# Sums of a weight pair ahead of its last parts, conversion steps of ScalarE one step later, other PSUM banks at both ends of the channel layer, one product moved

## Chip, cores and metric

One core of one Trainium2 chip runs the whole program. The metric is the device time of one execution in microseconds (us), the median of several runs.

## The reference, cut to what matters

Three layers follow each other: attention with a computed position bias, a token and channel mixer, and a gated mixer. The change lies in the second and in the conversion of weights around it.

```python
def _moe_ref(x, w_tok1, w_tok2, w_ch1, w_ch2):        # x: 4 x 576 x 512
    xt = x.transpose(0, 2, 1)
    h = np.maximum(xt @ w_tok1, 0.0) @ w_tok2          # token mixing, 576 -> 256 -> 576
    u = x + h.transpose(0, 2, 1)
    h2 = np.maximum(u @ w_ch1, 0.0) @ w_ch2            # channel layer, 512 -> 1536 -> 512
    return u + h2
```

The third layer, `_moe2_ref`, begins with `x @ w_in` and ends with `@ w_out`.

## The kernel before

**Numbers in two parts.** Every large product works on operands that are split into a high part (rounded to the matmul format `F32R`) and a low part (the remainder). A product is three matmuls for each 128 rows of contraction: high by high, high by low, low by high. ScalarE (ACT) makes the high part by a cast, VectorE (DVE) the low part by a subtraction.

**Weights.** They come as 64-bit numbers. `Jobs` (L70) converts them, one block of 128x512 at a time, while the products run. A job is a row of pieces: the square of the upper word on ScalarE (L158, into the one buffer `sq`), then four steps of DVE on the words (L159, L165, L170, L175), of which L175 reads `sq`. Between these steps stand the high part (`finish`, L122 on ScalarE) and the low part (`subtract`, L132 on DVE) of the job before. `piece()` issues one such step; `work(k)` issues k of them at fixed places of the channel layer, and `wjobs.limit` says how far they may run ahead. `need(key)` issues what is missing at once. Each engine works off its own queue in order.

**The channel layer** runs over 2304 columns of `X`, as a first double of 2 x 512 columns with 256 more beside it (`d0`, `small=True`) and a second double of 2 x 512 columns (`d1`). A double goes over the 1536 hidden features in six pairs of blocks of 128, in three groups of two; below they are called pair 0 to pair 5 (n in `Double.run`, L1350). A pair uses seven half products in place of eight, in a scheme after Strassen and Winograd: on the weights' side it wants the blocks themselves (`wa`, `wq`, `wb`) and four sums of them (`wsum`, made by `sum_steps`, L969, with the name `ws`), on the columns' side four mixed blocks M1 to M4 (`mixer`, L1470: subtractions of DVE, then casts of ScalarE and subtractions of DVE again) and M22.

In a pair n > 0 of the first double TensorE (PE) runs, in this order: the product of `wa` with the first half of u into bank `ma`, which ScalarE copies to `s1` (L1370); the product with the second half into `mb`, which DVE adds to `s1` (L1386); the product of `ws` (S2) with M2, added to `ma`, which ScalarE copies (L1390); the 256 columns (`up256`, L1260); S1 with M1 into `mb` (up to pair 4, and in pair 5 too before the change); S3 with M3 into `ma`, copied by L1411; M4 into `ma`; the 256 columns' second product (`down256`, L1281, banks `my` and `mx`); S4 with M22. Between them stand the second products of the pair before (`down1`, L1228, into four banks `a`). In pairs 2 and 4, where a group begins, the group before is closed: `close` adds its sums to `X` (L1236), and `other` runs the second products of its other half, from the parts that `relu` makes (L1070 on ScalarE, L1074 on DVE). Pair 0 has code of its own (`pair0`, L1327).

The bodies `hooks0` and `hooks1` say at which places of a pair the mixers, the weight pieces and the fetches come. SyncE (SP) issues all DMAs: the loads of the raw weights (two buffers), the stores of `wa`, `wb` and `ws` to DRAM for the second double (L953), and their fetches.

**Around it.** Token mixing of the last batch ends with products `pu` (L1099), which DVE adds to `X` (L1104). The gated mixer begins with products `pv` (L1615).

Of the kernel before, what the change touches and what calls it, by code (L numbers as in the profile page):

```python
# [19 lines left out]
def kernel(ctx, tc, ins, consts, out, dbg=None, nb=4, stop=None):  # L20
# [49 lines left out]
    class Jobs:  # L70


        def __init__(self, stg, ahead):
            self.stg, self.ahead = stg, ahead
            self.queue, self.loaded, self.next, self.open, self.gen = [], {}, 0, None, None
            self.done = set()
            self.rest = None
            self.lnext, self.limit, self.last = 0, None, {}
# [57 lines left out]
        def parts(self):  # L136

            self.load()
            key, src, wd, dst, times = self.queue[self.next]
            self.next += 1  # L140
            if src is None:
                for i, step in enumerate(dst):
                    if i > 0:
                        yield
                    step()
                self.done.add(key)
                return
            raw = self.loaded.pop(self.next - 1)
            n = src.shape[1] * src.shape[2]
            r = slice(0, src.shape[0] * times)  # L150
            if wd:
                w = self.stg.tile([P, WMAX], F32, tag="w", name="w", bufs=2)
                sq = self.stg.tile([P, WMAX], F32, tag="sq", name="sq", bufs=1)
                self.subtract()
                up_, dn = raw[r, 0:n, 1], raw[r, 0:n, 0]
                wf = w[r, 0:n]
                wi_ = wf.bitcast(I32)
                S.activation(out=sq[r, 0:n], in_=up_.bitcast(F32), func=AF.Square)  # L158
                V.tensor_scalar(  # L159
                    out=wi_, in0=up_, scalar1=0x07FFFFFF, scalar2=3,  # L160
                    op0=ALU.bitwise_and, op1=ALU.logical_shift_left,
                )
                yield
                self.finish()
                V.scalar_tensor_tensor(  # L165
                    out=wi_, in0=up_, scalar=-0x40000000, in1=wi_, op0=ALU.bitwise_and, op1=ALU.bitwise_or
                )
                yield
                self.subtract()
                V.scalar_tensor_tensor(  # L170
                    out=wi_, in0=dn, scalar=29, in1=wi_, op0=ALU.logical_shift_right, op1=ALU.bitwise_or
                )
                yield

                V.scalar_tensor_tensor(  # L175
                    out=wf, in0=sq[r, 0:n], scalar=THR * THR, in1=wf, op0=ALU.is_ge, op1=ALU.mult
                )
            else:
                self.finish()
                self.subtract()  # L180
                wf = raw[r, 0:n]
            self.open = (key, wf, dst)
            self.last[key] = wf
# [782 lines left out]

    S1, S3, S4, S2 = range(4)

    def sum_steps(j):  # L969
# [17 lines left out]
        def one():  # L987
            wjobs.finish()
            new_s(j)
            raw.append(stg.tile([P, WMAX], F32, tag="sq", name="sq").rearrange("p (o a b) -> p o a b", o=2, a=ND2))  # L990
            (a11, a12), (a21, a22) = w(2 * j), w(2 * j + 1)
            add(0, a21, a22, ALU.add)
            add(1, a11, a21)
            hi(S1)

        def two():
            wjobs.subtract()

        def three():
            lo(S1)  # L1000
            (a11, a12), (a21, a22) = w(2 * j), w(2 * j + 1)
            add(1, raw[0][:, 0], a11)
            add(0, a12, raw[0][:, 1])
            hi(S4)
            if j < NJ - 2:
                keep("a", j, wa[j])
                keep("b", j, wb[j])

        def four():
            lo(S4)  # L1010
            if j < NJ - 1:
                keep("s", j, wsum[j])

        return [one, two, three, four]

# [200 lines left out]
    with tc.tile_pool(name="ps_ch", bufs=1, space=PSUM, reuse_waits="tile") as pc:  # L1216
# [73 lines left out]
        class Double:  # L1290
# [36 lines left out]
            def pair0(self):  # L1327

                (j, j1), a, b = self.groups[0], bank("ma"), bank("mb")
                for ps, w, m in ((a, [wa[j][:, i] for i in range(2)], (M1, M2)), (b, None, (M1, M2))):  # L1330
# [18 lines left out]

            def run(self, hooks, first=False, small=False, banks=("ma", "ma", "mb", "mb"), end=None):  # L1350

                self.small, self.hooks = small, hooks
                seq = [(g, j) for g in self.groups for j in g]
                for n, (group, j) in enumerate(seq):
# [15 lines left out]
                    S.copy(out=s1, in_=a)  # L1370
                    step(k_)
                    if da:
                        self.down1(pj, 0, pgrp, range(ND) if small or begins else range(ND2))
                    step(k_)
# [16 lines left out]
                    step(k_)  # L1391
                    if da and not small and not begins:
                        self.down1(pj, 0, pgrp, range(ND2, ND))
                        relu(s1, gs[0])
# [5 lines left out]
                    if begins:  # L1400
# [5 lines left out]
                        else:  # L1406
                            self.other(acc, lst, 1, k_)
                    c = bank(banks[3])
                    product(c, ws_(S1), M1, start=True)
# [14 lines left out]
                    elif n > 0:  # L1424
                        self.down1(pj, 1, pgrp)
                        step(1)
                    product(a, [wb[j][:, i] for i in range(2)], M4)
                    relu(a, gs[1])
                    hooks(n, "P4")
                    if sm and not begins:  # L1430
                        down256(j)
                        relu(s1, gs[0])
                    elif not sm and not begins and (small or not da):
                        relu(s1, gs[0])
# [23 lines left out]
                acc = [bank(nm) for nm in end] if end else new_acc()  # L1458
                for k in range(len(lst)):
                    self.other(acc, lst, k, self.pieces if k + 1 < len(lst) else 0)  # L1460
                    build()
                add_up(acc, self.c0 + CK)

# [29 lines left out]
        def hooks0(n, where):  # L1493
            if where == "start":
                wjobs.limit = base + 5 * (n + 1) + 1
            if where == "up":
                wjobs.limit = base + 5 * (n + 1) + 2
            if n == 0 and where == "others":
                mixer(3, raws(), 0)
                for i in range(2):  # L1500
                    S.copy(out=M22[i], in_=M2[i].bitcast(F32))
                mixer(2, raws(), 0)
            if n == 0 and where == "C21":
                wjobs.limit = base + 8
                work(8)
                mixer(1, slots[2:4], 0)
            if where == "P3":
                wjobs.limit = base + 5 * (n + 1) + 5
                work(4 if n > 0 else 0)
            if n == 0 and where == "P3":  # L1510
                mixer(4, raws(), 0)
            if n < NJ - 1:
                return
            if where == "P7":
                u_parts(D1, u0)
                for i in (3, 2, 4, 1):
# [29 lines left out]

        d0.run(hooks0, first=True, small=True)
        fetch("s", order1[0], new_s(order1[0], 1))
        d1.run(hooks1, banks=("ma", "my", "mb", "mx"), end=("ma", "mb", "mx", "my"))
    mxr.release()  # L1550
# [328 lines left out]
```

## Time and profile before

| what | us |
|---|---|
| median of 3 runs (877.66 to 879.55) | 877.88 |
| the profiled execution | 878.13 |
| its span, first to last instruction | 876.3 |
| PE busy | 848.7 (97%) |
| DVE busy | 698.6 (80%) |
| ScalarE busy | 457.0 (52%) |

The channel layer lies from 358 to 661 us of the span; the first double's pairs 1 to 5 begin with their first product at 375, 403, 438, 458 and 493 us, the second double at 537 us. A busy share of PE says little of what is to be had; its idle time and what ended it is the view to begin with, then the granted clock behind each such wait, then the queue of the engine that ended it.

### The profile page before, as it was taken

Reading aid. Unit: us, or ns where it says so; the run is one execution under the profiler, and the core shown is the slowest. Engines: PE = TensorE matmul, PEld = TensorE weight load, DVE = VectorE, ACT = ScalarE, POOL = GpSimd, SP = SyncE. Lnnn points to the kernel's source line nnn. Section 1 sums busy time; section 2 is a strip of 40 time slices with the busy share of each in tenths; the row PEclk is TensorE's granted clock in tenths of the full one; section 3 lists DMA queues with packets and bytes.
Section 4 is the critical chain, followed back from the end, with each engine's and each line's share of the span. In section 5 each row is a group of like instructions: output and inputs, shape, how many; then the busy total and the mean of one; then the engine's idle time right before and its main releaser. Section 6 shows DMA issues by size and latency. Waiting matters only on the chain.

```text
span 876.3 us, 21629 instructions
## 1 busy us (share of the span) xinstructions
PE 848.7 (97%) x8608; PEld 704.3 (80%) x8608; DVE 698.6 (80%) x1526; ACT 457.0 (52%) x996; POOL 231.8 (26%) x440
## 2 busy tenths in 40 slices
PE   9999999999999999969999899999998999999998
PEld 4466788888888888858787777888877989889997
DVE  7899788888887789589798876467578989988756
ACT  7999888888888635343343333123244522322310
POOL 1345567676766200000000000000003322322230
PEclk9999999999999999989999999999999999999999
DMA  7965544444432132044343010435025001010002
GB/s 190 190 141 132 133 92 77 81 93 87 90 70 62 57 108 97 1 147 165 97 157 120 24 49 26 144 111 202 15 78 109 25 1 49 1 61 1 1 13 97
DMA packets 127732, 74.30 MB, mean 85 GB/s; under 512 B 104592, under 2 KB 112912, under 8 KB 126352
## 3 DMA queue, kind: packets, MB, share of 16 engines
q1 hardware_dynamic: 127472, 72.79, 32.0%
q8 instruction: 68, 1.11, 0.5%
q14 instruction: 32, 0.26, 0.1%
q10 hardware_dynamic: 160, 0.13, 0.1%
HBM read 47.01 MB, written 13.11 MB: 69 GB/s over the span
## 4 chain that ended last, share of the span: by engine, by line
PE 53%; DVE 7%; ACT 2%; issue 1%; DMA 0%; DVEq 0%; ACTq 0%; SPq 0%
PE a L1228 11%; PE ps L1690 6%; PE pu L1668 6%; PE pv L1615 6%; PE po L1721 6%; PE ma L1064 5%; PE mb L1064 3%; PE my L1064 2%; PE mx L1064 2%; PE pu L1099 2%; PE mx L1260 1%; PE ph L674 1%; DVE g L1074 1%; DVE X L1236 1%; PE mx L1281 1%; DVE w L170 1%
## 5 line engine op out<-in xcount | busy, mean ns | idle before, releaser
L530 POOL TENSOR_SCALAR pr<-pr,sm 128x576 f32<-128x576 f32 (+2 forms) x208 | 130.7, 646 | 46.0 <-DVE sm L523 37.8
L1228 PE MATMUL a<-g,c 128*128 128x512 f32 x528 | 125.7, 390 | 1.6 <-ACT c L122 1.3
L1228 PEld LDWEIGHTS a<-g,c 128*128 128x128 f32 x528 | 98.7, 188 | 23.1 <-ACT c L122 1.5
L516 ACT ACTIVATE pr<-pr,mn 128x576 f32<-128x576 f32 x144 | 112.3, 780 | 6.7 <-DVE mn L503 4.2
L503 DVE CUSTOM_DVE_ANT_0 pr<-ss,bias_m 128x576 f32<-128x576 f32 x128 | 94.5, 750 | 19.3 <-PE ss L497 17.4
L63 POOL TENSOR_TENSOR y<-X,y 128x576 fp32r<-128x576 f32 x4 | 7.0, 1787 | 366.0 <-DMA wsr<-in_moe_w_sg_dram 366.0
L597 PEld LDWEIGHTS o<-xA,vm 64*64 64x64 f32 x1280 | 69.9, 133 | 11.1 <-issue 5.4
L597 PE MATMUL o<-xA,vm 64*64 64x128 f32 (+1 forms) x1280 | 78.8, 261 | 0.0
L1183 DVE STREAM_TRANSPOSE res<-X 32x256 f32<-32x256 f32 (+1 forms) x176 | 68.2, 387 | 2.8
L598 PE MATMUL o<-yA,vm 64*64 64x128 f32 x1024 | 68.0, 272 | 0.0
L497 PE MATMUL ss<-kt,X 64*64 64x288 f32 x816 | 66.8, 410 | 0.0
L158 ACT ACTIVATE sq<-wraw 128x512 f32<-128x512 f32 (+2 forms) x43 | 28.2, 655 | 56.7 <-DVE w L175 38.5
L598 PEld LDWEIGHTS o<-yA,vm 64*64 64x64 f32 x1024 | 56.4, 133 | 0.4
L1690 PE MATMUL ps<-wsT,vn 128*128 128x288 f32 x384 | 56.4, 295 | 0.0
L374 DVE TENSOR_SCALAR X<-ttab,wsm 128x576 f32<-128x576 f32 x108 | 55.3, 572 | 0.1
L1690 PEld LDWEIGHTS ps<-wsT,vn 128*128 128x128 f32 x384 | 52.7, 188 | 0.3 <-POOL vn L63 0.2
L1668 PEld LDWEIGHTS pu<-y,c 128*128 128x128 f32 x384 | 51.3, 188 | 0.3
L1668 PE MATMUL pu<-y,c 128*128 128x288 f32 x384 | 51.5, 294 | 0.0
L573 PE MATMUL x<-ident,pr 128*128 128x128 f32 x320 | 47.0, 273 | 0.0
L1721 PE MATMUL po<-u,gm 128*128 128x512 f32 x192 | 44.0, 389 | 0.0
L1721 PEld LDWEIGHTS po<-u,gm 128*128 128x128 f32 x192 | 36.0, 188 | 7.4
L63 POOL TENSOR_TENSOR gm<-uT,gm 128x512 fp32r<-128x512 f32 x16 | 23.3, 1454 | 70.0 <-ACT gm L62 70.0
(257 smaller groups left out, 1977.0 us busy)
## 6 DMA issues: line engine op xcount, KB each, us to landing
wraw<-in_moe_w_ch_dram SPq DMA_DIRECT2D x24, 512.0 KB, 3.6
bias_m<-bst SPq DMA_DIRECT2D x32, 288.0 KB, 3.9
s<-ws SPq DMA_DIRECT2D x5, 1024.0 KB, 4.2
ws<-s SPq DMA_DIRECT2D x5, 1024.0 KB, 5.6
vm<-in_v_dram SPq DMA_DIRECT2D x32, 128.0 KB, 3.1
wraw<-in_moe_w_in_dram SPq DMA_DIRECT2D x8, 512.0 KB, 3.8
out_dram<-res SPq DMA_DIRECT2D x16, 256.0 KB, 2.1
kr<-in_k_dram SPq DMA_DIRECT2D x48, 72.0 KB, 3.0
```

Of the source, the lines that this page charges most:

```text
L497: T.matmul(ss[a % na][o, hf, 0:HN], lhsT=ql, rhs=kr_, start=True, stop=True)
L503: V.tensor_tensor_reduce(out=pr[:, a * NB:a * NB + N].rearrange("p (f n) -> p f n", f=2), in0=ss[a][:, :, 0:HN], in1=bias[a].rearrange("p ...
L516: S.activation(out=pr[:, a * NB:a * NB + N], in_=pr[:, a * NB:a * NB + N], func=AF.Exp, scale=-1.0, bias=mn[:, a:a + 1], accum_out=sm[:, a ...
L530: G.tensor_scalar(out=pr[:, dc:dc + hi - lo], in0=pr[:, lo:hi], scalar1=sm[:, a:a + 1], scalar2=1.0, op0=ALU.mult, op1=ALU.mult,)
L597: T.matmul(o[0:HD, 0:w], lhsT=vm[r, t, 0], rhs=xs[r, t, 0:w], start=st_, stop=en)
L598: T.matmul(o[HD:P, 0:w], lhsT=vm[r, t, 1], rhs=rh[r], start=st_, stop=en)
L1064: T.matmul(ps, lhsT=w[i][:, d], rhs=x[j][:, d], start=start and d == 0 and n == 0, stop=stop and d == ND2 - 1 and n == 2, skip_group_check ...
L1183: V.transpose(out=o, in_=src(c)[32 * a:32 * a + 32])
L1228: T.matmul(acc[d], lhsT=c2[f][i][:, d * P:(d + 1) * P], rhs=g[:, j], start=start and m == 0, stop=stop and m == 2,)
L1668: T.matmul(pu[:, hf, 0:HN], lhsT=wi[i][0][d][:, f * P:(f + 1) * P], rhs=y[j][:, d, js], start=d == 0 and m == 0, stop=d == ND - 1 and m == 2,)
L1690: T.matmul(ps[:, hf, 0:HN], lhsT=vn[i][:, t, ds_], rhs=wsT[j][:, t, js], start=t == 0 and m == 0, stop=False,)
L1721: T.matmul(po[:, cs], lhsT=g[i][:, d, gs], rhs=wo[j][d][:, cs], start=d == 0 and m == 0, stop=d == NG - 1 and m == 2,)
```

## The change

- `sum_steps` has five steps in place of four. The two sums and their high and low parts come first; the high parts (`finish`) and low parts (`subtract`) of `wq` and `wb` come after them. The store of the sums is issued ahead of the stores of `wa` and `wb`.
- From the channel layer on (`wjobs.late`), ScalarE's square is issued with the second step of DVE in place of the first, `finish` with the third in place of the second, `subtract` ahead of the fourth in place of the third.
- At the start of pair 0 all pieces up to the sums of pair 1 are issued, then mixer 3. Mixer 4 moves to pair 1, behind the addition to `s1`.
- The four `a` banks are named first (`new_acc` in `pair0`). They come to lie in PSUM banks 0 to 3 and `ma`, `mb` in 4 and 5; before, `ma` and `mb` lay in 0 and 1, the `a` banks in 2 to 5. The last `pu` of token mixing lies in 4 and 5 in both, and the four buffers of `pv` in 0 to 3.
- In pair 5, S1 goes into bank `mx` in place of `mb`, and half of the `down1` that stood ahead of the second product stands behind S2 (`two`). `need` for the last second-layer block is called at the place P7.
- The last of the four second products of the first double's other half, with its addition to `X`, is handed to the second double, which runs it in its first pair ahead of M4 (`fill`).

```diff
@@ Jobs.parts
-                S.activation(out=sq[r, 0:n], in_=up_.bitcast(F32), func=AF.Square)
+                square = lambda: S.activation(out=sq[r, 0:n], in_=up_.bitcast(F32), func=AF.Square)
+                if not self.late:
+                    square()
...
-                self.finish()
+                late = self.late
+                if late:
+                    square()
+                else:
+                    self.finish()
...
-                self.subtract()
+                if late:
+                    self.finish()
+                else:
+                    self.subtract()
...
+                if late:
+                    self.subtract()
@@ sum_steps
         def one():
-            wjobs.finish()
             new_s(j)
...
         def two():
-            wjobs.subtract()
-
-        def three():
             lo(S1)
...
+        def three():
+            lo(S4)
+            if j < NJ - 1:
+                keep("s", j, wsum[j])
+            summed.add(j)
+
+        def four():
+            wjobs.finish()
+
+        def five():
+            wjobs.subtract()
             if j < NJ - 2:
                 keep("a", j, wa[j])
                 keep("b", j, wb[j])
@@ Double.pair0
+                self.acc = new_acc()
                 (j, j1), a, b = self.groups[0], bank("ma"), bank("mb")
@@ Double.run
+                    two = da and not sm and not begins
                     if da:
-                        self.down1(pj, 0, pgrp, range(ND) if small or begins else range(ND2))
+                        self.down1(pj, 0, pgrp, range(ND2) if two else range(ND))
...
-                    if da and not small and not begins:
+                    if two:
                         self.down1(pj, 0, pgrp, range(ND2, ND))
                         relu(s1, gs[0])
...
-                    c = bank(banks[3])
+                    c = bank(banks[3] if sm else "mx")
...
+                    elif fill is not None:
+                        fill()
                     product(a, [wb[j][:, i] for i in range(2)], M4)
...
-                for k in range(len(lst)):
-                    self.other(acc, lst, k, self.pieces if k + 1 < len(lst) else 0)
+                for k in range(len(lst) - 1):
+                    self.other(acc, lst, k, self.pieces)
                     build()
-                add_up(acc, self.c0 + CK)
+
+                def rest():
+                    self.other(acc, lst, len(lst) - 1)
+                    add_up(acc, self.c0 + CK)
+
+                return rest
@@ hooks0
             if where == "start":
                 wjobs.limit = base + 5 * (n + 1) + 1
+                if n == 0:
+                    wjobs.limit = base + 8
+                    while 1 not in summed:
+                        wjobs.piece()
+                    mixer(3, raws(), 0)
+            if n == 1 and where == "P2":
+                mixer(4, raws(), 0)
...
             if n == 0 and where == "others":
-                mixer(3, raws(), 0)
...
             if n == 0 and where == "C21":
-                wjobs.limit = base + 8
-                work(8)
+                work(2)
                 mixer(1, slots[2:4], 0)
...
-                work(4 if n > 0 else 0)
-            if n == 0 and where == "P3":
-                mixer(4, raws(), 0)
+                work(5 if n > 0 else 0)
...
             if where == "P7":
+                wjobs.need(("c2", NF - 1))
...
+        wjobs.late = True
+        rest = d0.run(hooks0, first=True, small=True)
```

**ScalarE between pair 0 and pair 1.** `g` are the parts of relu, `wq` and `wb` the second block's high parts, `ws` the sums' high parts, `m` the mixers' high parts (from `cs`: mixer 1, from `scratch`: mixer 4), `s` the copy of the first product of pair 1. Before:

```order
L1070 ACTIVATE g_6599<-mx 128x512
L1070 ACTIVATE g_6600<-ma 128x512
L122 CAST wq<-w 128x256
L122 CAST wb<-w 128x256
L981 CAST ws<-sq 128x512 x2
L1466 CAST m_6017<-cs_6603 128x512
L1466 CAST m_6017<-cs_6604 128x512
L1466 CAST m_6607<-scratch 128x512 x2
L1370 COPY s_6019<-ma 128x512
```

And now:

```order
L1084 ACTIVATE g_6596<-mx 128x512
L1084 ACTIVATE g_6597<-ma 128x512
L122 CAST wq<-w 128x256
L122 CAST wb<-w 128x256
L1489 CAST m_6017<-cs_6600 128x512
L1489 CAST m_6017<-cs_6601 128x512
L1385 COPY s_6019<-ma 128x512
L158 ACTIVATE sq<-wraw 128x512 x2
L1489 CAST m_6604<-scratch 128x512 x2
L1406 COPY cs_6600<-ma 128x512
```

The casts of the sums are gone from here (they stand ahead of pair 0's copies), and the copy to `s` stands ahead of mixer 4's casts.

**DVE in pair 5**, from the addition to `s1` on; `c` are low parts of second-layer weights, `u` those of the second double's columns, `cs` what L1412 and L1436 add up. Before:

```order
L1386 TENSOR_TENSOR s_6019<-mb,s_6019 128x512
L132 TENSOR_TENSOR c_10_5988<-w,c_10_5987 128x512
L170 SCALAR_TENSOR_TENSOR w<-wraw,w 128x512
L175 SCALAR_TENSOR_TENSOR w<-sq,w 128x512
L1412 TENSOR_TENSOR cs_6604<-mb,cs_6604 128x512
L63 TENSOR_TENSOR u_5960<-X,u_5959 128x512 x4
```

And now:

```order
L1402 TENSOR_TENSOR s_6019<-mb,s_6019 128x512
L179 SCALAR_TENSOR_TENSOR w<-wraw,w 128x512
L132 TENSOR_TENSOR c_10_5988<-w,c_10_5987 128x512
L185 SCALAR_TENSOR_TENSOR w<-sq,w 128x512
L1088 SCALAR_TENSOR_TENSOR g_6596<-s_6019,g_6596 128x512
L1428 TENSOR_TENSOR cs_6601<-mx,cs_6601 128x512
L132 TENSOR_TENSOR c_11_5990<-w,c_11_5989 128x512
L63 TENSOR_TENSOR u_5960<-X,u_5959 128x512 x4
```

The relu of `s1` and the low part of the last second-layer block come earlier, and the sum is read from `mx`.

## Rows read from the trace of the kernel before

**Rows 1.** Page, part 1: engine, busy us (share of span), instructions.
```profile
PE 848.7 (97%) x8608; PEld 704.3 (80%) x8608; DVE 698.6 (80%) x1526; ACT 457.0 (52%) x996; POOL 231.8 (26%) x440
```
**Rows 2.** PE's waits, whole span: tile, line, releaser: us in total, times, longest.
```profile
PE ma L1064 <- ACT s L1370: 8.3, 1, 8.3
PE mb L1064 <- DVE s L1386: 2.3, 1, 2.3
PE pv L1615 <- DVE X L1236: 2.3, 1, 2.3
PE my L1281 <- DVE c L132: 1.8, 2, 0.9
...
PE a L1228 <- ACT c L122: 1.3, 1, 1.3
PE my L1281 <- ACT g L1070: 1.2, 2, 0.8
...
PE px L658 <- DVE x L63: 0.8, 1, 0.8
...
PE ma L1064 <- ACT cs L1411: 0.7, 1, 0.7
```
**Rows 3.** Stretches: length; busy of PE, PEld, DVE, ACT, POOL; PEclk; DMA share; GB/s.
```profile
360.40:421.30 60.90, 51.01 (x273) 43.74 (x271) 50.04 (x88) 25.65 (x45) 0.00 (x0) 0.94 0.37 121
...
386.20:389.00 2.80, 2.77 (x7) 2.22 (x8) 2.63 (x6) 0.55 (x1) 0.00 (x0) 0.50 0.00 0
...
502.50:505.30 2.80, 2.75 (x7) 2.17 (x8) 1.89 (x3) 0.03 (x1) 0.00 (x0) 0.50 0.00 0
...
520.10:523.40 3.30, 3.19 (x13) 2.34 (x14) 2.71 (x5) 0.00 (x0) 0.00 (x0) 1.00 0.78 303
```
**Rows 4.** PE in order of time: start, us, line, out<-in [idle before <-releaser].
```profile
358.32 2.93 PE L1064 MATMUL ma<-m,wa 128*128 128x512 f32 x12
...
372.14 1.60 PE L1281 MATMUL my<-g,c 128*128 128x256 f32 x12
...
386.23 2.93 PE L1064 MATMUL ma<-m,ws 128*128 128x512 f32 x6 [8.30 <-ACT s L1370]
...
423.72 1.55 PE L1064 MATMUL mb<-m,ws 128*128 128x512 f32 x6
...
502.55 2.92 PE L1064 MATMUL mb<-m,ws 128*128 128x512 f32 x6 [2.27 <-DVE s L1386]
505.28 1.82 PE L1064 MATMUL ma<-m,ws 128*128 128x512 f32 x6
...
520.12 3.38 PE L1228 MATMUL a<-g,c 128*128 128x512 f32 x12 [1.25 <-ACT c L122]
...
544.75 1.66 PE L1064 MATMUL ma<-m,wb 128*128 128x512 f32 x6 [0.68 <-ACT cs L1411]
...
663.60 11.22 PE L1615 MATMUL pv<-c,u 128*128 128x512 f32 x48 [2.25 <-DVE X L1236]
```
**Rows 5.** DVE in order of time, same columns.
```profile
359.13 0.75 DVE L1104 TENSOR_TENSOR X<-pu,X 128x576 f32<-128x576 f32 x1
...
407.88 0.69 DVE L985 TENSOR_TENSOR ws<-sq,ws 128x512 fp32r<-128x512 f32 x1 [0.69 <-ACT ws L981]
...
420.61 0.68 DVE L132 TENSOR_TENSOR c<-w,c 128x512 fp32r<-128x512 f32 x1
```
**Rows 6.** ScalarE in order of time, same columns.
```profile
365.53 2.00 ACT L1501 CAST m<-m 128x1024 fp32r<-128x1024 f32 x2
...
385.60 0.58 ACT L1370 COPY s<-ma 128x512 f32<-128x512 f32 x1
...
497.43 0.58 ACT L1370 COPY s<-ma 128x512 f32<-128x512 f32 x1
```
**Rows 7.** Groups of instructions, 360 to 421 us: count | busy, mean ns | idle before.
```profile
L132 DVE TENSOR_TENSOR wq<-w,wq 128x256 fp32r<-128x256 f32 x2 | 0.8, 420 | 0.0
```
**Rows 8.** The same view, 380 to 700 us: ScalarE's squares.
```profile
L158 ACT ACTIVATE sq<-wraw 128x512 f32<-128x512 f32 x29 | 19.6, 675 | 40.8 <-DVE w L175 35.3 <-issue 4.4 <-DVE ws L985 1.1
```

More of the change, by code (lines that the diff above doesn't have):

```diff
@@ L73, in __init__ @@
         def __init__(self, stg, ahead):
-            self.stg, self.ahead = stg, ahead
+            self.stg, self.ahead, self.late = stg, ahead, False
             self.queue, self.loaded, self.next, self.open, self.gen = [], {}, 0, None, None
@@ L967 @@
     S1, S3, S4, S2 = range(4)
+    summed = set()
     def sum_steps(j):
@@ L1007, in three @@
                 keep("b", j, wb[j])
[L1009 to L1014, printed above, removed]
+        return [one, two, three, four, five]
     def c1_jobs(j):
@@ L1348, in pair0, with run @@
                 self.hooks(0, "P3")
-            def run(self, hooks, first=False, small=False, banks=("ma", "ma", "mb", "mb"), end=None):
+            def run(self, hooks, first=False, small=False, banks=("ma", "ma", "mb", "mb"), end=None, fill=None):
                 self.small, self.hooks = small, hooks
@@ L1432, in run @@
                         relu(s1, gs[0])
-                    elif not sm and not begins and (small or not da):
+                    elif not sm and not begins and not two:
                         relu(s1, gs[0])
@@ L1545, in hooks1 @@
                 y0.extend(u_parts(0, u0))
-        d0.run(hooks0, first=True, small=True)
+        wjobs.late = True
+        rest = d0.run(hooks0, first=True, small=True)
         fetch("s", order1[0], new_s(order1[0], 1))
-        d1.run(hooks1, banks=("ma", "my", "mb", "mx"), end=("ma", "mb", "mx", "my"))
+        d1.run(hooks1, banks=("ma", "my", "mb", "mx"), end=("ma", "mb", "mx", "my"), fill=rest)()
     mxr.release()
```

## The prediction

> **What bounds the kernel now.** The page's busy times come first: PE is busy for 848.7 us, 97% of the span [rows 1], so only its waits and its clock are left to win. The second view is the list of what PE waited for [rows 2]. Its longest, 8.3 us, lies between pair 0 and pair 1. Other waits are 2.3 us in pair 5, 2.3 us at the first `pv`, two kinds at `down256` and one each at a `down1`, a `px` and an M4 product. The third view is the granted clock behind the long ones [rows 3]: 0.50 (1.2 GHz) after the 8.3 us and again after the 2.27 us in pair 5, but 1.00 (2.4 GHz) after a wait of 1.25 us [rows 3, 4]. Six matmuls that take 1.55 us at 2.4 GHz take 2.93 and 2.92 there, and the next six in pair 5 1.82 [rows 4]: about 1.7 us more at each place. The fourth view is the queue of the engine that ended each wait, below.
>
> **Pairs 0 to 2: the long wait.** PE waits for `ma`, which ScalarE has not copied. ScalarE copies at 385.60 [rows 6], because ahead of it in its queue stand the casts of mixers 1 and 4, and these wait for DVE, which works on weights and sums first. In the changed order the copy stands ahead of mixer 4, and sums and mixer 3 are done while PE runs pair 0, so this wait goes entirely. What is late next is DVE: it is left with the same work, and PE cannot pass `down256` of pair 2 before the low part of c that starts at 420.61 [rows 5]. So I count the gain at that point, on DVE. It is free for the weights at 360.4, half a microsecond behind the last addition of `pu` [rows 5]; up to 421.3 it is busy 50.0 of 60.9 us [rows 3], so 10.9 us are gaps.
>
> In the changed order these gaps remain: four waits for a sum's cast, 0.69 each [rows 5], 2.8 us, two of them new since `wq` and `wb` no longer fill them; and some 1.6 us ahead of mixer 2's low parts, because its casts stand on ScalarE behind the M22 casts of 2.00 us [rows 6], and these behind mixer 3's casts and pair 0's two copies. About 1.2 us of small gaps stay. Two operations of 0.6 us are added to the stretch (one step of pair 1's second block, once done before it, and the step that now stands ahead of the last c subtraction). So 10.9 - 2.8 - 1.6 - 1.2 - 1.2 = 4.1 us. Walking the queue row by row, with the spacings of the rows, gives 5.0, since neighbours that follow without a wait overlap a little. I take **4.6 us**, bounds 3 and 5.5. PE's new small waits within these pairs (for the 256 columns' relu in pair 0, for the c12 copy behind mixer 4's casts in pair 1, for a relu part and for c in pair 2, 0.5 to 1.3 us each) are part of this count and cost nothing more.
>
> **The bank at the start.** `ma` now lies where the last `pu` lay, so the first product, at 358.32 [rows 4], waits for its addition from 359.13 to 359.88 [rows 5]: 1.5 us. Nothing is charged: DVE's chain above does not hang on that product, and PE would wait later, ahead of `down256` at 372.14 [rows 4], for mixer 2 and the relu anyway. Without that cover it costs the 1.5 us.
>
> **One step later, pairs 3 and 4.** Of ScalarE's idle time ahead of the squares, 35.3 us ended with L175 of DVE [rows 8]: each square stands at the head of the queue until DVE frees its buffer. Behind it wait copies and relus for PE. One step later the buffer is free when the square's turn comes. That takes most of the 1.2 us that PE waits for ScalarE at `down256` in pairs 2 and 4 [rows 2]. Against it, the low part of c comes one operation (0.6 us) later, and PE's last wait there, 1.8 us in two [rows 2], is for just this; and `wq` and `wb` (two subtractions of 0.42 us [rows 7], spaced 0.35) now follow the sums in place of filling a wait, 0.7 us more of DVE per pair. In pair 3 I find a new wait of 0.25 us for the addition to `s1`, in pair 4 the last part of c 0.5 us later than now. Sum: **0.75 us lost**, bounds 2.0 lost and 1.2 won. In the second double and the gated mixer the same shift costs nothing, for PE waits for nothing of the conversions there [rows 2]; without that cover it is 0.6 us for each block.
>
> **Pair 5.** S1 no longer needs `mb`, so the wait of 2.27 us for L1386 goes with its clock: 2.27 + 1.4 + 0.3. The last second-layer block is finished at P7, early enough to end the 1.25 us for ScalarE's cast, after which the twelve matmuls took 3.38 in place of 2.9 [rows 4]: 1.25 + 0.5. Against it, PE reaches S2 earlier by the half `down1` (six matmuls, 1.36 us) that moved behind it, while the copy, at 497.43 [rows 6], comes some 0.6 us later behind the casts of `wq` and `wb`: a wait of 1.3 us, of which the moved matmuls give all but 0.6 back afterwards. **5.1 us won**; bounds 3.5 (the clock falls after that wait) and 5.7.
>
> **Into the second double.** The last second product of `d0` runs between S3 and M4, so M4 no longer waits 0.68 us for its copy, and 0.1 us of clock goes [rows 4]: **0.8 us won**, bounds 0.5 and 0.8. DVE waits for PE in this stretch; the additions that are put off have their place there.
>
> **The banks at the end.** `pv` took banks of `ma` and `mb`, whose last additions DVE makes late. Now it takes banks 0 to 3, those of `a`, free since the group was closed. All of the 2.25 us [rows 4] goes: **2.2 us won**, bounds 1.5 and 2.4. What follows (`bn_stats`, the norms) is paced by `pv` and shifts with it.
>
> **Token mixing.** There too sums come ahead of `wq` and `wb`, and DVE reaches the last `x` of batch 3 some 0.5 us earlier; PE waits 0.82 us for it [rows 2]. **0.5 us won**, bounds 0 and 0.8.
>
> **DMA.** On SP the store of the sums passes the stores of `wa` and `wb`. The next raw load stands behind all three as before and waits for a buffer that DVE frees later than that. Nothing.
>
> **Sum.** 4.6 - 0.75 + 5.1 + 0.8 + 2.2 + 0.5 = 12.45 us. The profiled execution took 878.13, its span 876.3, the median of the runs is 877.88, 0.25 less; against its own time the sum gives 878.13 - 12.45 = **865.7 us**.
>
> **Rivals.**
>
> The clock falls at the waits that are left. Three of them are not covered by DVE's count: `down256` in pairs 2 and 4, and S2 in pair 5, with single waits of 1.2 to 1.3 us, in pairs 2 and 4 two or three close to each other. At the price of rows 4, 1.4 to 1.7 us each, that is 4.2 to 5.1 us: about 870.4. For it speak the two places with 0.50, against it the 1.00 after 1.25 us [rows 3], which is the size of those I expect. [...] 18%.
>
> The first gain does not come. If DVE's chain from 360.4 on hangs on PE after all (the bank's 1.5 us at the start, passed on through pair 0's copies on ScalarE to mixer 2), the 4.6 us shrink to 0 or a little above: 870 to 871. For it: DVE is the bound of that stretch and all of the cover argument is about its queue; against: the sums and mixer 3 need nothing of pair 0's products. 13%.
>
> Squares too late, slower than before. Say ScalarE, behind a copy that waits for PE, starts a square more than 0.7 us after DVE's second step has started. Then L175 waits for the copy (0.58 us [rows 6]) and the square (0.675 us [rows 8]), and PE waits for DVE: a ring of three queues. The 19 conversions that are left in the first double would cost up to 19 x 1.25 = 23.8 us: 889.5. It decides from 12.45 / 19 = 0.65 us per conversion, where it eats the sum. Against it: a square needs nothing but the raw block and the buffer, and some 1.3 us lie between the two steps of DVE. 4%.
>
> The waits only change their place, each term at its lower bound or worse, within 0.2% of now: 3%.
>
> **How the numbers follow.** The forecast, with its terms between their bounds (863 to 869), has 62%, the four rivals 18, 13, 4 and 3%. The likeliest time is 865.7. For 8 in 10 the range takes in the forecast's own and most of the clock's and the first gain's case: 863.0 to 870.8. About 0.2% is what a measurement of this kernel can tell from no change; faster by more than that 0.92, within it 0.03, slower 0.05.
>
> **What would show it.** In the changed profile: no PE wait for the copy to `s` ahead of S2 in pair 1; a new wait of about 1.5 us at the first `ma`, for L1104's successor; in pair 2 PE waits in pieces of about 1 us for DVE's relu and c parts, with the clock at 1.00 (at 0.50 the first rival is right); no wait for `mb` and full clock in pair 5, but one of about 1.3 us ahead of S2 there; none ahead of the second double's first M4, none ahead of `pv`. Squares should no longer stand behind L175. If L175 waits for squares, or if PE passes `down256` of pair 2 less than 3 us earlier than now, the working is wrong at that step.

## The result and the profile after

The changed kernel takes 866.95 us (median of 4 executions, 865.76 to 869.26) against 878.71 in the same rounds: a ratio of 0.9859, 95% interval 0.9818 to 0.9901. Run again later, 867.28 (6 executions, ratio 0.9862, 0.9836 to 0.9887). The forecast was 865.7, with 863.0 to 870.8 as the range. The profiled execution took 865.76, its span 863.7 us.

The page of the kernel after, parts 1 and 2 (compare [rows 1]; 40 equal slices, tenths, PEclk the granted clock):

```profile
PE 845.2 (98%) x8608; PEld 701.7 (81%) x8608; DVE 697.2 (81%) x1526; ACT 454.9 (53%) x997; POOL 230.7 (27%) x440
...
PEclk9999999999999999999999999999999999999999
```

No engine has less work to do; PE is busy 3.5 us less, with the clock full all through. The rest are waits. PE's waits from 318 to 680 us after the change (compare [rows 2]; tile, line, releaser, us, times, longest):

```profile
PE my L1295 <- DVE g L1088: 3.0, 3, 1.3
PE my L1295 <- DVE c L132: 2.1, 2, 1.1
PE a L1242 <- DVE g L1088: 1.9, 2, 1.0
PE ma L1078 <- DVE X L1118: 1.5, 1, 1.5
PE ma L1078 <- ACT s L1385: 1.1, 1, 1.1
PE ma L1078 <- ACT cs L1406: 0.4, 1, 0.4
```

Lines of the changed kernel are some 14 higher: L1078 is the product, L1295 `down256`, L1242 `down1` and `other`, L1088 and L1084 the low and high part of a relu, L1385 the copy to `s1`. Gone are the 8.3 us ahead of pair 1's S2, the 2.3 us for `mb`, the 2.3 us at `pv`, the 1.3 us for ScalarE's cast and the 0.7 us at M4. New are 1.5 us for the bank at the start and waits of about 1 us for DVE in pairs 2 and 4. PE in pair 2 (start, us, [idle before <-releaser]); pair 4 has the same three waits, 0.93, 1.24 and 1.07:

```profile
409.35 2.79 PE L1242 MATMUL a<-g,c 128*128 128x512 f32 x11 [0.98 <-DVE g L1088]
...
413.53 0.74 PE L1295 MATMUL my<-g,c 128*128 128x256 f32 x4 [1.28 <-DVE g L1088]
415.33 1.10 PE L1295 MATMUL my<-g,c 128*128 128x256 f32 x7 [1.06 <-DVE c L132]
416.27 1.60 PE L1295 MATMUL mx<-g,c 128*128 128x256 f32 x12
417.70 1.55 PE L1078 MATMUL mb<-m,ws 128*128 128x512 f32 x6
```

Where the time came from is read off PE at fixed products, before and after. "Ahead" is how much earlier the product starts now, "term" what was won or lost since the row above:

| product | before | after | ahead | term | forecast |
|---|---|---|---|---|---|
| `pu`, mid of token mixing | 320.58 | 320.02 | 0.56 | chance: 319.93 to 320.86 in the kernels run here | none |
| last `pu` | 351.93 | 350.59 | 1.34 | token mixing 0.8 | 0.5 |
| S1 of pair 2, behind `down256` | 423.72 | 417.70 | 6.02 | pairs 0 to 2: 4.7 | 4.6 |
| first product of pair 5 | 493.18 | 489.10 | 4.08 | pairs 3, 4: -1.9 | -0.75 |
| last products of `d0` | 526.21 | 516.88 | 9.33 | pair 5: 5.3 | 5.1 |
| pair 1 of the second double | 547.61 | 537.39 | 10.22 | 0.9 | 0.8 |
| first `pv` | 663.60 | 650.99 | 12.61 | banks at the end 2.4 | 2.2 |

### The profile page after: what moved, and what is told of

It reads as the page before. It is cut to its first block, busy times and chain, and to the rows that moved or that the text cites. A ratio compares the mean times of both kernels' runs of the same rounds, so it can differ in the third digit from the quotient of the medians.

```text
span 863.7 us, 21638 instructions
## 1 busy us (share of the span) xinstructions
PE 845.2 (98%) x8608; PEld 701.7 (81%) x8608; DVE 697.2 (81%) x1526; ACT 454.9 (53%) x997; POOL 230.7 (27%) x440
## 3 DMA queue, kind: packets, MB, share of 16 engines
q8 instruction: 68, 1.11, 0.6%
## 4 chain that ended last, share of the span: by engine, by line
PE 83%; DVE 12%; ACT 2%; issue 2%; DMA 1%; SPq 0%; ACTq 0%; DVEq 0%
PE a L1242 10%; PE ss L507 9%; PE ps L1718 6%; PE pu L1696 6%; PE po L1749 6%; PE pv L1643 6%; PE o L607 5%; PE x L583 4%; PE ma L1078 4%; PE y L588 3%; PE bps L403 3%; PE ph L684 3%; PE o L608 3%; PE mx L1078 2%; PE pu L1113 2%
## 5 line engine op out<-in xcount | busy, mean ns | idle before, releaser
L1242 PE MATMUL a<-g,c 128*128 128x512 f32 x528 | 126.2, 390 | 1.9 <-DVE g L1088 1.9
L1242 PEld LDWEIGHTS a<-g,c 128*128 128x128 f32 x528 | 98.7, 188 | 23.6 <-DVE g L1088 3.2
```

The lines of the kernel that those rows point to most:

```text
L1242: T.matmul(acc[d], lhsT=c2[f][i][:, d * P:(d + 1) * P], rhs=g[:, j], start=start and m == 0, stop=stop and m == 2,)
```

## Experiments

Each is the changed kernel but for the edit shown. Executions of one kernel differ by how often the granted clock falls to 0.50, so two kernels are compared at the same mean clock, or by PE's place with the falls taken out.

**What a fall costs, and how often.**

> The changed kernel once more, on the same chip and in the same rounds as the two above: a span of 863.7 where the clock is full, and about 1.7 us more for each stretch at half clock in pairs 2 or 4; the median of the executions about 867, as before, if the clock falls in most of them at these waits.

The waits are the same as in the first profile to 0.05 us, but here the clock fell behind them: it is 0.50 from 415.4 to 418.4 us. PE in pair 2, and the stretches 413 to 417 and 417 to 421 us (length; PE, PEld, DVE, ACT, POOL; PEclk; DMA):

```profile
413.40 0.74 PE L1295 MATMUL my<-g,c 128*128 128x256 f32 x4 [1.24 <-DVE g L1088]
415.21 1.86 PE L1295 MATMUL my<-g,c 128*128 128x256 f32 x7 [1.07 <-DVE c L132]
416.86 2.34 PE L1295 MATMUL mx<-g,c 128*128 128x256 f32 x12
419.04 1.55 PE L1078 MATMUL mb<-m,ws 128*128 128x512 f32 x6
...
413.00:417.00 4.00, 2.53 (x12) 2.33 (x13) 3.09 (x6) 0.42 (x1) 0.00 (x0) 0.77 0.44 119
417.00:421.00 4.00, 4.00 (x22) 3.65 (x21) 2.05 (x3) 0.63 (x1) 0.00 (x0) 0.81 0.11 44
```

The 19 `down256` matmuls take 4.20 in place of 2.70 us: 1.5 us. Of the ten executions of this kernel two had a mean clock of 1.0 (spans 863.2 and 863.7), seven 0.998 (864.7 to 866.6), one 0.996 (867.2). So the median holds about one such fall, which the sum of the prediction did not.

**The start, alone.** The kernel before with the order of sums and mixers at the start, and nothing else:

```diff
+ sum_steps: sums, hi, lo of a pair ahead of wq, wb
+ start of pair 0: while 1 not in summed: wjobs.piece(); mixer(3, raws(), 0)
+ pair 1, "P2": mixer(4, raws(), 0)
```

> The kernel before with one part of the change alone: the sums ahead of wq and wb, all weight steps up to the sums of pair 1 and mixer 3 at the start of pair 0, mixer 4 in pair 1. Banks, conversion steps, pair 5 and the product handed on are as before. Theory: the 8.3 us wait ahead of pair 1's S2 goes, and its stretch at half clock, but DVE bounds the stretch up to pair 2, so that PE passes down256 of pair 2 only 3.5 to 4.7 us earlier than before (the shift of the conversion steps, which is not in this kernel, gave about 1 of the 4.7 in pair 1); pairs 3 and 4 then lose 2 to 2.6 us, and pair 5 and the first pv wait as before: a span of 874 to 875 against 876.3, so 876 to 877. Rival: the wait was a loss of PE's own and the whole of 8.3 + 1.7 us comes: a span of 866 to 867.

878.52 us against 879.64 in the same rounds, ratio 0.9986 (0.9967 to 1.0006): no difference. The 8.3 us are gone, yet nothing is left of them. PE's waits, first lines, 318 to 680 us:

```profile
PE mb L1078 <- DVE s L1401: 2.9, 1, 2.9
PE my L1295 <- ACT g L1084: 2.7, 3, 0.9
PE pv L1641 <- DVE X L1250: 2.2, 1, 2.2
PE a L1242 <- DVE g L1088: 2.2, 3, 1.0
```

Against the kernel before PE is 0.84 us ahead at 358, 4.76 at `down256` of pair 2 (so 3.9 won, as expected), 3.41 behind a fall there, 0.74 at the end of pair 4 (2.7 lost), and 0.07 in pair 5, where the wait for `mb` is 2.9 in place of 2.27. It loses about what was expected; the fall in pair 2 came on top. The median lies above the expected 876 to 877; the two executions at a mean clock of 0.998, the fullest here, took 876.57 and 877.10. The rival, 10 us won, is out: PE's wait of 8.3 us was mostly DVE's lag in another place.

**Mixer 4 back behind pair 0.**

```diff
-            if n == 1 and where == "P2":
+            if n == 0 and where == "P3":
                 mixer(4, raws(), 0)
```

> The changed kernel with mixer 4 back behind pair 0, ahead of pair 1's copy to s1. Theory (DVE's queue counts, not the place of PE's wait): the copy stands behind mixer 4's casts again and PE waits some 2 us ahead of S2 of pair 1, but passes down256 of pair 2 within 0.5 us of where it does now, since the waits there shrink by as much: 863.5 to 864.2 of span at full clock, and 1.7 more if the clock falls at the new wait. Rival: PE's own wait is added to the rest; then PE passes down256 of pair 2 about 2 us later and the span is 865.7 at full clock.

The wait is there, and the clock fell on it: the rows of PE in pair 1 are

```profile
381.26 2.31 PE L1078 MATMUL ma<-m,ws 128*128 128x512 f32 x6 [1.80 <-ACT s L1385]
383.37 2.50 PE L1274 MATMUL mx<-x,wa 128*128 128x256 f32 x12
```

PE is then up to 3.7 us late, but at `down256` of pair 2 only 1.6. At equal clock the spans agree: 865.8 at 0.998 (the changed kernel 864.7 to 866.6), 866.6 at 0.996 (867.2). Of the wait itself nothing shows at the end; the 1.6 us is about the size of the fall. With two executions, and another fall in pair 4 of the profiled one, wait and fall can't be separated in this run.

**The conversion steps, back at their old place.**

```diff
-        wjobs.late = True
```

> The changed kernel with the conversion's square, cast and subtraction at their old steps; all else as changed (865.8 in its profiled execution, PE behind down256 of pair 4 at 475.3, behind the others after pair 5 at 516.9). Theory: the shift is worth little by itself. Undone, the subtraction of c stands one DVE operation (0.6 us) earlier, and the squares stand at the head of ScalarE's queue again and give back up to 1.2 us of waits in pairs 2 and 4. 865.2 to 866.6, PE behind pair 4 within 0.6 of 475.3. Rival one: the shift is what made pairs 3 and 4 lose 1.95 us, so undoing it wins 1.2 to 2: 863.8 to 864.6, PE behind pair 4 at 473.3 to 474.1. Rival two: the shift carries the early copies (a copy behind a square that waits is late), so undoing it costs 2 to 4 us: 868 to 870, with ScalarE's waits for the last conversion step as long as in the kernel before.

870.26 us; 868.65 with the clock full all through, a span of 866.6 against 863.7. My theory fell, and the second rival is right: the shift is worth 2.9 us. 0.9 is lost in pair 1, 0.6 in pair 3, 0.5 in pair 5, 0.6 in the gated mixer, tenths elsewhere. ScalarE in pair 1, first with the old steps, then of the changed kernel:

```profile
387.71 0.67 ACT L158 ACTIVATE sq<-wraw 128x512 f32<-128x512 f32 x1 [2.25 <-issue]
388.29 0.58 ACT L1084 ACTIVATE g<-mx 128x512 fp32r<-128x512 f32 x1
388.77 0.61 ACT L122 CAST c<-w 128x512 fp32r<-128x512 f32 x1
```

```profile
385.78 0.60 ACT L1084 ACTIVATE g<-mx 128x512 fp32r<-128x512 f32 x1
387.49 0.67 ACT L158 ACTIVATE sq<-wraw 128x512 f32<-128x512 f32 x1 [1.11 <-issue]
388.06 0.61 ACT L122 CAST c<-w 128x512 fp32r<-128x512 f32 x1
```

With the old steps the relu stands behind a square that waits for its buffer and comes 2.5 us later than with the new ones; the cast of c comes 0.7 later, and DVE waits 0.71 us for it.

**wq and wb fill the wait again, from pair 2 on.**

```diff
 def one():
+    if j > 1: wjobs.finish()
 def two():
+    if j > 1: wjobs.subtract()
```

> The changed kernel, but from pair 2 on the casts of wq and wb stand ahead of the sums again and their subtractions fill the wait for the sums' first cast; pair 1 keeps the new order. Theory: DVE is the bound from pair 0 to the end of pair 4, so each unfilled wait of 0.69 to 0.73 us is lost for good: in pairs 2, 3 and 4 together 2.1 us come back, PE behind down256 of pair 4 at 473.2 in place of 475.3, and the copy that S2 of pair 5 waits for (1.1 us) comes about 0.6 earlier. Time 863.0 to 863.8. Rival: the loss in pairs 3 and 4 comes from the subtraction of c, which stands one operation later; then nothing comes back, 865.5 to 866.1, and PE passes pair 4 at 475.3 as now.

PE gains 0.66 us in pair 2, 0.70 in pair 4 and 0.62 in pair 5, together 2.0 us, and loses 0.2 in pair 3; the theory had 2.1 by the end of pair 4 and 0.6 in pair 5. And the last two waits at `down256` stayed at 2.35 us in either pair, the clock fell behind both, and DVE's wait for a load in pair 3 (below) grew to 2.39 us. In its one execution with the clock full it takes 864.62, against 865.28 and 865.76 of the changed kernel and above the expected 863.0 to 863.8; its median, 867.35, is no better.

**The store of wa early.**

```diff
 def one():
     hi(S1)
+    if j < NJ - 2: keep("a", j, wa[j])
 def five():
-    keep("a", j, wa[j])
```

> The changed kernel, but the store of wa is issued in the first step of the sums, as early as it can be, in place of behind the store of the sums. Theory: pairs 3 and 4 lost 1.95 us and not 0.75 because DVE waits 1.56 us at 444.9 for a raw block whose load stands behind 1.75 MB of stores. Without it DVE reaches the end of pair 4 some 1.2 to 1.5 us earlier and PE, whose waits in pair 4 are all for DVE, passes down256 of pair 4 at 474.0 in place of 475.3, against the same point of pair 2. A span of about 862.4 where the granted clock is full throughout, and each stretch at half clock about 1.7 more. Rival: DVE's wait is covered by the slack at the start of pair 4, where it waits for PE; then nothing changes, 863.7 at full clock, and the loss lies in the sums' casts alone.

Four views: DVE in pair 3 of the changed kernel; SP's queue in the kernel before (stores L953, loads L108); SP in the changed kernel (stores L963); and SP with the early store.

```profile
444.89 0.43 DVE L161 TENSOR_SCALAR w<-wraw 128x512 int32<-128x512 int32 x1 [1.56 <-DMA wraw<-in_moe_w_ch_dram]
```

```profile
430.24 0.42 SPq L953 DMA_DIRECT2D a<-wa  x1
439.60 0.33 SPq L953 DMA_DIRECT2D b<-wb  x1
442.66 0.32 SPq L953 DMA_DIRECT2D s<-ws  x1
444.49 4.03 SPq L108 DMA_DIRECT2D wraw<-in_moe_w_ch_dram  x2
```

```profile
436.63 0.33 SPq L963 DMA_DIRECT2D s<-ws  x1
437.01 0.42 SPq L963 DMA_DIRECT2D a<-wa  x1
437.53 0.85 SPq L963 DMA_DIRECT2D b<-wb  x1
439.14 8.03 SPq L108 DMA_DIRECT2D wraw<-in_moe_w_ch_dram  x3
```

```profile
426.04 0.33 SPq L963 DMA_DIRECT2D a<-wa  x1
438.76 0.33 SPq L963 DMA_DIRECT2D s<-ws  x1
439.44 0.32 SPq L963 DMA_DIRECT2D b<-wb  x1
441.27 6.47 SPq L108 DMA_DIRECT2D wraw<-in_moe_w_ch_dram  x3
```

In the kernel before, wa's store left SP at 430.24, some 9 us ahead of the next one. Behind the sums it left with them, and the load followed 1.75 MB of stores. With the early store the wait of 1.56 is gone. From the first product of pair 3 to the end of `down256` of pair 4 PE takes 42.3 us in place of 43.7: 1.5 us won, nearly all of it in pair 4, as the theory had it. The median is 867.02: two of its four executions have a mean clock of 0.996, so nothing of it shows there. At 0.998 its spans are 864.3 and 864.5 against 865.1 to 865.4 in five of the changed kernel's seven (864.7 and 866.6 in the other two).

**The old banks.**

```diff
     def pair0(self):
-        self.acc = new_acc()
```

> The changed kernel with the old PSUM banks (ma, mb in 0 and 1). Theory: the wait of 1.5 us at the first product goes, but DVE's chain of pairs 0 to 2 does not hang on it, so PE passes down256 of pair 2 at 417.7 as now; the wait of about 2.25 us at the first pv comes back. 868.0, PE at pv about 2.2 us later than 651.0. Rival: the start's wait is paid in full; then PE passes pair 2 at 416.2 and the time is 866.5.

869.63 us. The 1.54 us at the start are gone, and PE waits in pair 0 instead: 0.33 for a copy and 0.89 + 0.53 at `down256`, in place of 0.52, so that it passes that point no earlier:

```profile
373.40 0.39 PE L1295 MATMUL my<-g,c 128*128 128x256 f32 x1 [0.89 <-ACT g L1084]
374.32 1.58 PE L1295 MATMUL my<-g,c 128*128 128x256 f32 x11 [0.53 <-DVE g L1088]
```

From the last `pu` to the end of this `down256` PE takes 25.9 us with either banks. So the wait at the start was covered. The wait at `pv` is back, 1.61 us. At a clock of 0.998 its spans are 867.1 and 867.6, 1.9 and 2.4 us above the typical 865.2.

**Pair 5 as before.**

```diff
-                    c = bank(banks[3] if sm else "mx")
+                    c = bank(banks[3])
-                    two = da and not sm and not begins
+                    two = da and not small and not begins
-                wjobs.need(("c2", NF - 1))
```

> The changed kernel with pair 5 as before: S1 into mb, all of the down1 ahead of the second product, the last second-layer block not forced at P7. Theory: the 5.25 us that pair 5 won come from there alone: a wait of about 2.3 us for the addition that frees mb, the granted clock at 0.50 behind it, and about 1.2 us for ScalarE's cast ahead of M4's relu come back: 870.5 to 871.2, with PE behind the others after pair 5 at 522. Rival: the order of sums and the later steps have already moved those waits; then 1 to 3 us come back, with the clock at 1.00: 867 to 869.

873.93 us. PE's rows:

```profile
504.21 2.93 PE L1078 MATMUL mb<-m,ws 128*128 128x512 f32 x6 [2.89 <-DVE s L1402]
506.93 1.87 PE L1078 MATMUL ma<-m,ws 128*128 128x512 f32 x6
...
521.81 3.37 PE L1242 MATMUL a<-g,c 128*128 128x512 f32 x12 [1.25 <-ACT c L122]
```

Both waits and the half clock are back as the theory had it. From the end of pair 4 to the end of pair 5 PE loses 5.9 us, 0.7 above the forecast, since the wait for `mb` is 2.89 and not 2.27. The other 5.2 us to the 874.8 of its profiled span are falls in pairs 2 and 4 (4.3) and a start 0.8 later; such falls, on top of the one in pair 5, put the median above what was expected. At a mean clock of 0.998 its span is 870.2.

**DVE's waits filled, then other banks, then the order in pairs 2 and 4.** Three steps towards a better kernel. The first joins the two edits above with two in pair 0:

```diff
 start of pair 0:
+    for i in range(2): S.copy(out=M22[i], in_=M2[i].bitcast(F32))     # was ahead of mixer 2
+    mixer 3's raw sums and casts between the first and second step of pair 1's sums,
+    its low parts between the second and third
```

> The changed kernel with DVE's known waits filled: subtractions of wq and wb in the wait for the sums' first cast from pair 2 on; in pair 0 mixer 3 between the steps of pair 1's sums (two waits of 0.69); the M22 casts of 2.0 us ahead of pair 0, where ScalarE is idle for 7.65 us, in place of ahead of mixer 2's casts (a wait of 1.49); the store of wa early (a wait of 1.56 for a load in pair 3). Theory: DVE is the bound from 360 to the end of pair 4, so 1.3 + 1.4 + 0.7 come by the end of pair 2 (PE there at about 414.5 in place of 417.7, its waits of 3.3 us nearly gone), and 1.5 + 0.7 more by the end of pair 4 as far as PE still waits there (3.2 us); pair 5's wait for the copy shrinks by 0.6. Span 858 to 859.5 with the clock full, as no long waits are left for it to fall at. Rival one: the bank's wait of 1.5 us at the first product is no longer covered, so about 1.5 less is won: 859.5 to 861. Rival two: other waits (ScalarE's parts, loads) take the place, 861 to 862.5.

863.64 us, 860.1 and 861.0 of span at full clock: some 3 us won where 4 to 5.5 were expected, which is the level of the first rival. The waits at `down256` were still 2.3 and 2.1 us. A head start of DVE alone doesn't end them. Then the banks:

```diff
                 self.acc = new_acc()
+                bank("mx"), bank("my")
                 (j, j1), a, b = self.groups[0], bank("ma"), bank("mb")
```

> The kernel fill_all with the banks named in the order a, mx, my, ma, mb, so that ma and mb lie in banks 6 and 7, which nothing holds at the start. Theory: with DVE's waits filled the first product's wait of 1.5 us is no longer covered, so this wins up to 1.5 us over fill_all: 857 to 858.5 with the clock full. Rival: it is still covered by ScalarE's and DVE's work ahead of down256 in pair 0; then the two are the same within 0.3 us.

862.28 us, 859.3 at full clock, about 1.3 less than fill_all. From the last `pu` to the end of `down256` of pair 0 PE takes 23.3 us in place of 25.1: with DVE's waits filled the first product's wait is no longer covered, as the theory said, though the level is higher than expected. Then the order:

```diff
 in pairs 2 and 4, behind the copy to c12:
-    step(3)
+    step(2); wjobs.finish()
 behind up256(j):
-    step(1)
+    step(0)
 behind relu_lo_256():
+    wjobs.subtract()
-    self.other(acc, lst, 0, 3)
+    self.other(acc, lst, 0, 5)
```

First on the changed kernel alone:

> The changed kernel with one thing more: in pairs 2 and 4 the low part of the pair's second c block is made as soon as its conversion ends, ahead of the next block's steps (one later step of two blocks stands behind it), instead of ahead of the next block's fourth step. Theory: the waits at down256 in pairs 2 and 4 (2.3 us each, for g and then c) come from the order on DVE, three steps of a block that nobody waits for standing ahead of the two rows that PE waits for; DVE has gaps of 2.0 and 1.7 us behind them, where those steps fit. So about 2.0 us come in each of the two pairs: PE behind down256 of pair 4 at 471.3 in place of 475.3, span 859.7 to 860.5, and the granted clock has no wait left in pairs 2 and 4 to fall at. Rival: DVE's total work is the bound up to the end of pair 4; then the steps that were put off cost the same later, pair 3 starts its sums later, and 0 to 1 us is left: 862.7 to 863.7 at full clock.

864.57 us. From the first product to the first `pv` PE wins 1.8 us, not 4: the waits at `down256` shrink from 2.3 to 1.2 us, and what is left is ScalarE, whose relu now stands behind the cast of c. PE in pair 2:

```profile
413.26 0.39 PE L1295 MATMUL my<-g,c 128*128 128x256 f32 x1 [0.88 <-ACT g L1084]
413.99 1.69 PE L1295 MATMUL my<-g,c 128*128 128x256 f32 x11 [0.34 <-DVE g L1088]
```

But the clock was at 0.999 or 1.0 in all four executions. On top of fill_banks:

> The kernel fill_banks with that same early low part in pairs 2 and 4. Theory: its gains (4.4 us at full clock over the changed kernel) and this one (up to 2.0 for each of pairs 2 and 4, as far as PE still waits there, 2.3 and 2.1 us) add up: span 855.0 to 857.0, time 857.0 to 859.0, clock full in nearly all executions. Rival: what was filled is then covered by PE, and only one of the two counts: span 858 to 859.5.

858.97 us (six executions, 858.44 to 859.22), ratio 0.9767 to the kernel before (0.9740 to 0.9793), 8.3 us below the changed kernel in the same rounds, and the clock at 0.999 or more in all six. That is within what was expected. It is the fastest kernel of this study, and the gains add. The first lines of its waits (lines stand some 6 higher again):

```profile
PE my L1301 <- ACT g L1090: 1.5, 2, 0.8
PE my L1301 <- DVE g L1094: 0.7, 2, 0.3
PE ma L1084 <- ACT cs L1413: 0.7, 1, 0.7
PE ma L1084 <- ACT s L1392: 0.5, 1, 0.5
```

## Why the prediction was right, and where it was not

**Pairs 0 to 2**, 4.6: measured 4.7. The count on DVE's queue was the right one: counted by PE's wait and its clock, the start alone should have won 10 us, and it won 3.9 there. Some 1.0 of the 4.7 hangs on the shift of ScalarE's steps (late_off), which the working of this term names only as a cost. PE waits in pair 2 for DVE in three pieces of about 1 us, as forecast, and DVE waits 1.49 us ahead of mixer 2's low parts where 1.6 were forecast.

**Pairs 3 and 4** are the mis-sized term: -0.75 forecast, -1.9 measured, at its bound. What failed is the step on DMA, "Nothing". It said that the raw load stands behind all three stores as before; it does, but wa's store had left long before the others, and now all three go together. DVE's 1.56 us for it, and the 1.5 us of PE that the early store gave back, more than cover the 1.2 us of difference; with them taken out some 0.5 us is lost, near the forecast. I followed each queue's order, and not when the entries in it leave.

**The shift of ScalarE's steps** was sized within pairs 3 and 4 alone, where undoing it costs 0.8 us. Over the whole kernel undoing it costs 2.9; that includes 0.9 in pair 1, 0.5 in pair 5 and 0.6 in the gated mixer, places where the prediction names no gain from it. Its mechanism was only half right: the buffer is often not free at the square's turn. The view of [rows 8] after the change:

```profile
L158 ACT ACTIVATE sq<-wraw 128x512 f32<-128x512 f32 x29 | 19.5, 671 | 27.6 <-DVE w L185 20.7 <-issue 4.1 <-DMA wraw<-in_moe_w_ch_dram 2.7
```

Of 35.3 us behind DVE's last step 20.7 are left, so the sign that squares no longer stand behind it did not come. What did go is PE's wait for ScalarE at `down256` in pairs 2 and 4, 1.2 us before, while the waits for DVE at the same place grew from 1.2 to 2.3 us in either pair. Against this gain the order of the sums costs 2.0 us in pairs 2, 4 and 5 where its casts' waits stay empty (sums_fill). In the kernel before, without the shift and the rest of the change, the start wins nothing by the end, so these parts of the sum don't simply add.

**Pair 5**, 5.1: measured 5.3, and 5.9 when undone. The new wait ahead of S2 is 1.11 us with the clock at 1.00. **Second double**, **banks at the end**: 0.9 and 2.4 for 0.8 and 2.2. **The bank at the start**: covered, as argued, and no longer so once DVE's other waits are filled.

**The total.** The profiled execution came within 0.1 us of the forecast, and that is luck: the 1.2 us too much lost in pairs 3 and 4 are made up by the 0.56 us of chance in the first row of the table and by tenths in the other terms, and it is one of the two executions in ten without a fall of the clock.

**The rivals.** That the clock falls at the waits that are left had 18%, as all or nothing at three places. It is neither: the profiled execution has no fall, most have about one, and the one of these with a profile has it in pair 2, at a price of 1.5 us. That is about the 1.25 us by which the median lies above the forecast. Eight of ten executions had a fall and two had none; the two profiles, one of either kind, have the same waits. The Trainium skill, page "TensorE: Matmul & The Clock Gate", section "HAM oscillation — how this bites in real kernels", tells of a kernel whose bursts of matmuls are shorter than the DMA waits between them and which falls back at every one. The waits here are for other engines and 1.3 us or less, so no run here shows the page's case. The other rivals did not come: the first gain came, and squares are not too late: DVE idles 0.6 us in all ahead of its last conversion steps between 358 and 700 us, 1.2 before.

## What to carry to other kernels

When a long wait is taken away from an engine that runs at 97%, count the gain on the queue of the engine that made it wait, up to the next place where both meet, and follow that queue past the stage: what it saved here it lost again two pairs later. A step that is moved takes its DMAs along, and what matters of them is when each one leaves, not only their order. Of two engines' rows, those that another engine waits for belong ahead of steps that nobody waits for, even where both engines have time.

## What was not expected of the hardware

The same kernel with the same waits, equal to 0.05 us, runs its `down256` of pair 2 at a granted clock of 1.00 in one execution and at 0.50 in another, 1.5 us slower. Each wait there is 1.3 us or less; three follow each other within 7 us. Where an edit cut the last two from 2.3 to 1.2 us, all ten executions (two kernels, one of them with the other edits too) kept a mean clock of 0.999 or 1.0. Which of the waits decides whether the clock falls is not shown. In sums_fill and stores_early, where the waits at `down256` stayed, PE won 2.0 and 1.5 us elsewhere and the medians did not move: their executions had a mean clock of 0.993 to 1.0 and of 0.996 to 0.998.
